# An mLSTM cell and tanh-shrink kernel: gates in three groups, one scaling of v, decay after the sum, transfers and weights in another order

## The chip, the cores and the metric

The kernel runs on one core of one Trainium2 chip. The metric is device time in microseconds (us) of that core, for one execution. A single-core program has no second core to compare with, so a run is called slow only where it lies over 1.5% above the fastest of its kernel. Medians below are of all runs, and a slow one among them is named; ratios, and the verdicts drawn from them, use fast runs alone. The engines are PE (TensorE), PEld (its weight loads), DVE (VectorE), ACT (ScalarE), POOL (GpSimd) and SP (SyncE, which only issues transfers here).

## The reference

An mLSTM cell over 768 tokens, 4 batches and 8 heads of 40, then x @ w_in, g = h - tanh(h), g @ w_out. Cut to what matters:

```python
for t in range(S):
    m_new = max(f_gate[t] + m, i_gate[t])
    f_stab, i_stab = exp(f_gate[t] + m - m_new), exp(i_gate[t] - m_new)
    m = m_new
    C = f_stab * C + i_stab * outer(v[t], k[t])
    n = f_stab * n + i_stab * k[t]
    y[t] = sigmoid(o_gate[t]) * (C @ q[t]) / max(abs(n . q[t]), 1)
# x = y as [3072 tokens, 320 features]
h = x @ w_in                       # 320 x 2048
out = (h - tanh(h)) @ w_out        # 2048 x 320
```

## The kernel before

The sequence is cut into six chunks of 128 tokens. One chunk of one batch is a *unit*: 24 units, n = 4 x chunk + batch. A unit has, on PE, the scores (`ps`, k times q), the products inside the chunk (`ph` from `vs` and `P`), from the second chunk on the product with the carried state (`ph` from `state`), the update of that state (`pc`) and three transposes (`px`) that turn its result into columns of x. Two units make a group of 256 tokens for the large products: up (`ph_up`, x by w_in) and down (`po`, g by w_out). The weights come as 64-bit numbers and are converted to fp32 by DVE and ACT, block by block.

What is emitted for the first twelve units and the first up and down products is decided when the program is built, by a small planner. It holds a list of operations with estimated durations, ranks and dependences, always takes the one that can start first (the lower rank where two can), and emits it. Each engine then runs its instructions in the order emitted. So a wrong estimate costs nothing in correctness, but the engine stands in line behind the instruction that is late.

The planner fills what it believes to be PE idle time with *dummies* (`awake`, a bf16 product of 512 columns that nobody reads), meant to keep the array's clock up:

```python
def idle(t0, t1):
    n = int((t1 - t0) * 0.6 / 0.215)
    if n and not busy:
        awake(n)
```

The gates of chunk 0 are computed at once, those of chunks 1 to 5 together. Their rows lie in the x tiles of later groups:

```python
f_sb, i_sb, m_sb, lf = (... for t in xT[-4:])
load_gates(early)                  # chunk 0, first in the sync queue
...                                # kz, qz, v of two units; then o and k of two units
load_gates(later)                  # chunks 1 to 5
...
first_tokens, _ = gates(0, 1, -2.0, 3.6, in_small)
...
later_tokens, later_states = gates(1, NT, 1.5, 12.0, in_po)
```

v is scaled twice, once for the product inside the chunk and once for the state at its end; the old state is decayed first, and the update added with a mask for the pair of heads that share a product:

```python
scale = ei[:, both, t["c"], t["hs"]]                 # both = two scales
V.tensor_tensor(out=t["vs"][:, both, :, 0:D], in0=v, in1=scale, op=OP.mult)
V.tensor_tensor(out=new, in0=old, in1=eT[:, n, :], op=OP.mult)
...
for i in range(2):
    V.scalar_tensor_tensor(out=new, in0=pc, scalar=own[0:TOP, i:i + 1], in1=new, op0=OP.mult, op1=OP.add)
```

## Time and profile before

| | before |
|---|---|
| median of three runs | 571.06 us (568.33 to 571.93) |
| span of the profiled run | 570.1 us |
| PE busy | 551.2 us, 97% |
| DVE busy | 353.5 us, 62% |
| mean granted PE clock | 0.977 |
| bytes moved | 38.2 MB, 67 GB/s |

PE is the bound, so the number to work with is not its busy share, which counts waiting in the pipeline and half-clock passes as busy. It is the *loss*: the time up to some moment, less the work done by then at undisturbed rates (up product 4.52/24 us each, and so on, as the prediction lists them). Counted so from the trace, the loss before is 24.5 us at 50 us, 33.6 at 70, 33.8 at 100, 36.7 at 190 and 39.6 at the end. The prediction's count of 31.0 at 65.3 us credits PE with 2 us of gates as well, which the curve leaves out, and the last 6.7 us of the curve are the program's tail. Late in the program the curve falls (37.5 at 260 us, 33.0 when PE ends at 563.4), so the prediction's rates are a little too slow there, and losses of the late part are hidden; two kernels' curves can still be compared. The curve of each kernel is used below. Its steps are good to about one us, as an instruction counts when it ends.

### The profile page before, as it was taken

The numbers are of one execution on the slowest core, as the hardware profiler recorded it, in microseconds if no ns is written. First come the engines' busy times: TensorE is split into PE (matmuls) and PEld (weight loads), VectorE is DVE, ScalarE is ACT, GpSimd is POOL, SyncE is SP. The second block draws the span as 40 slices with busy tenths as digits, with TensorE's granted clock in tenths as the row PEclk, the third lists the DMA queues.
The fourth block names the chain that finished last, engine by engine and source line by source line (L and its number), as shares of the span: only waits on it lengthen the run. The fifth ranks groups of instructions, "written<-read, shape, count | busy, mean of one in ns | idle before, by whom it ended". The sixth has DMA issues, their size and how long they took to land.

```text
span 570.1 us, 9133 instructions
## 1 busy us (share of the span) xinstructions
PE 551.2 (97%) x3473; PEld 462.6 (81%) x3476; DVE 353.5 (62%) x769; ACT 179.2 (31%) x436; POOL 34.6 (6%) x69
## 2 busy tenths in 40 slices
PE   8788899999999999999999999999999999999995
PEld 4576687878877777689988988988988989988873
DVE  4789778788875425678656665665664555544421
ACT  2435343364242323313223222322322323232321
POOL 6230202320000000000000000000000000000000
PEclk9789799899999999999999999999999999999999
DMA  7985335453120000212122122111120000000000
GB/s 216 243 244 165 105 104 170 135 175 88 42 87 0 1 0 13 81 37 59 41 65 58 37 69 70 55 62 47 30 65 13 1 23 2 2 24 0 24 0 29
DMA packets 40194, 38.21 MB, mean 67 GB/s; under 512 B 3856, under 2 KB 37712, under 8 KB 40144
## 3 DMA queue, kind: packets, MB, share of 16 engines
q1 hardware_dynamic: 32712, 22.49, 13.7%
q0 software_dynamic: 3296, 10.82, 6.4%
q10 hardware_dynamic: 4136, 4.26, 2.1%
q8 instruction: 29, 0.48, 0.4%
q14 instruction: 21, 0.17, 0.1%
HBM read 33.62 MB, written 3.93 MB: 66 GB/s over the span
## 4 chain that ended last, share of the span: by engine, by line
PE 92%; DMA 3%; ACT 1%; DVE 1%; ACTq 1%; issue 0%; SPq 0%; DVEq 0%
PE ph_up L129 39%; PE pS L129 20%; PE po L129 16%; PE ph L129 9%; PE ps L129 4%; DMA qz<-in_qT 3%; PE pc L129 2%; PE px L133 2%; ACTq L106 1%; ACT q L106 0%; ACT z L106 0%; SPq L288 0%; DVE gt L106 0%; PE gate L129 0%; ACT L106 0%
## 5 line engine op out<-in xcount | busy, mean ns | idle before, releaser
L129 PE MATMUL ph_up<-xT,w_in 128*128 128x256 f32 (+1 forms) x1152 | 248.7, 394 | 2.0 <-ACT xT L106 1.1
L129 PEld LDWEIGHTS ph_up<-xT,w_in 128*128 128x128 f32 (+1 forms) x1152 | 170.4, 190 | 34.9 <-issue 12.2
L106 ACT ACTIVATE z<-ph_up 128x512 f32<-128x512 f32 (+1 forms) x100 | 57.1, 576 | 285.4 <-issue 156.4
L106 DVE SCALAR_TENSOR_TENSOR gt<-ph_up,z 128x512 f32<-128x512 f32 (+1 forms) x100 | 63.5, 663 | 103.0 <-ACT z L106 103.0
L129 PE MATMUL po<-w_out,gt 128*128 128x320 f32 x320 | 99.3, 455 | 2.5 <-DVE gt L106 2.0
L129 PEld LDWEIGHTS po<-w_out,gt 128*128 128x128 f32 x320 | 60.8, 198 | 29.5 <-issue 6.6
L106 DVE TENSOR_TENSOR P<-ps,upto 128x512 f32<-128x512 f32 x48 | 31.5, 684 | 62.3 <-PE ps L129 62.3
L106 ACT ACTIVATE q<-z,tiny 128x512 f32<-128x512 f32 (+1 forms) x100 | 64.9, 701 | 0.9 <-DVE gt L106 0.9
L106 DVE SCALAR_TENSOR_TENSOR gt<-q,gt 128x512 f32<-128x512 f32 (+1 forms) x100 | 63.1, 661 | 0.0
L129 PEld LDWEIGHTS ph<-vs,P 128*128 128x128 f32 x384 | 58.2, 194 | 4.2 <-ACT o L106 0.5
L129 PE MATMUL ph<-vs,P 128*128 128x41 f32 x384 | 57.2, 264 | 0.0
L129 PE MATMUL pS<-wT,s 128*128 128x160 f32 x336 | 52.0, 301 | 0.0
L129 PEld LDWEIGHTS pS<-wT,s 128*128 128x128 f32 x336 | 47.4, 190 | 0.0
L129 PE MATMUL pS<-w_out,gt 128*128 128x160 f32 x224 | 43.7, 315 | 0.0
L129 PEld LDWEIGHTS pS<-w_out,gt 128*128 128x128 f32 x224 | 32.7, 191 | 4.0 <-issue 3.3
L129 PE MATMUL ph<-state,q 80*128 80x82 f32 x160 | 31.4, 278 | 0.0
L129 PEld LDWEIGHTS ps<-qz,kz 40*128 40x128 f32 x384 | 25.4, 187 | 5.8 <-issue 4.0
L129 PE MATMUL ps<-qz,kz 40*128 40x128 f32 x384 | 27.2, 277 | 2.4 <-DMA qz<-in_qT 2.4
L129 PEld LDWEIGHTS ph<-state,q 80*128 80x128 f32 x160 | 26.4, 191 | 2.7 <-issue 0.3
L459 POOL DMA_DIRECT2D w<-in_moe_w_in x40 | 22.8, 576 | 73.5 <-DVE w_e L106 25.2
L106 ACT COPY xT<-px 128x384 f32<-128x384 f32 x24 | 11.4, 476 | 47.6 <-PE px L133 47.6
L129 PEld LDWEIGHTS pc<-vs,k 128*80 128x80 f32 x160 | 19.9, 172 | 3.4 <-issue 0.5
(92 smaller groups left out, 458.5 us busy)
## 6 DMA issues: line engine op xcount, KB each, us to landing
w<-in_moe_w_out POOLq DMA_DIRECT2D x16, 320.0 KB, 4.2
kz<-in_kT SPq DMA_DIRECT2D x48, 80.0 KB
o<-in_o_gate SPq DMA_DIRECT2D x24, 160.0 KB
k<-in_k SPq DMA_DIRECT2D x24, 160.0 KB
out<-ob ACTq DMA_DIRECT2D x24, 160.0 KB
qz<-in_qT SPq DMA_DIRECT2D x44, 80.0 KB
v<-in_v SPq DMA_DIRECT2D x22, 160.0 KB
q<-in_qT SPq DMA_DIRECT2D x40, 80.0 KB
```

Of the source, the lines that this page charges most:

```text
L106: i = method(*args, **kwargs)
L129: return cls.keep(nc.tensor.matmul(*args, **kwargs))
L133: return cls.keep(nc.tensor.transpose(*args, **kwargs))
L459: queue.dma_start(out=to[rows, cols], in_=part)
```

## The change

Its intent: let the first products start earlier, spread the gates, take work off DVE, and let the planner know what dummies and transfers really take. Cut to its core:

```diff
-        LAG = {"T": 0.25, "V": 0.07, "A": 0.12, "S": 1.7, "G": 1.9}
-        RATE = 0.23
+        LAG = {"T": 0.25, "V": 0.07, "A": 0.12, "S": 1.7, "G": 1.9, "N": 1.7}
+        RATE, SHARED = 0.25, 32.4
 ...                                  (each queue has its own transfer time in the plan)
-    f_sb, i_sb, m_sb, lf = (... for t in xT[-4:])
+    f_sb, i_sb, m_sb, lf = (... for t in (w_out[:, 2 * KEPT:], w_in[:, KEPT:]) for i in range(2))
-    load_gates(early)
+    load_gates(0, 2)
-    for name in "ok":
-        for n in range(2):
-            load_unit(n, (name,))
-    load_gates(later)
+    for n in range(2):
+        load_unit(n, ("o",))
 ...
+    CHUNKS = (0, 1, 2, NT)
 ...                                  ("until", "end" and "to end" are gone)
-        V.tensor_tensor(out=t["vs"][:, both, :, 0:D], ...two scales...)
+        V.tensor_tensor(out=to[:, :, 0:D], in0=t["v"], in1=scale..., op=OP.mult)
 ...
-                V.scalar_tensor_tensor(out=new, in0=pc, scalar=own[0:TOP, i:i + 1], in1=new, op0=OP.mult, op1=OP.add)
+            V.tensor_tensor(out=new, in0=pc, in1=old, op=OP.add)
+        V.tensor_tensor(out=new, in0=new if t["c"] else pc, in1=decay, op=OP.mult)
 ...
+    plan_gates(0, -2.0, 3.3, in_small)
+    plan_gates(1, -1.64, 3.3, in_po)
-    later_tokens, later_states = gates(1, NT, 1.5, 12.0, in_po)
+        if n == 2 * B:
+            plan_gates(2, 1.17, 30.0, in_po)
 ...
-            op = plan.add("G", 1.2 if k else 2.8, fetch, (), r, [("w64", held)], at=at, kb=655)
+            op = plan.add("S" if k else "G", 1.5 if k else 2.8, fetch, (), r, [(buffer, held)], at=..., kb=655)
 ...
-        n = int((t1 - t0) * 0.6 / 0.215)
+        n = int((t1 - t0) * 0.9 / 0.43 if t0 < 6.0 else (t1 - t0) * 0.4 / 0.215)
```

Ranks of units and weight blocks change too. The second ring for w_out exists only in the plan: the transfers themselves are still issued by GpSimd.

## The prediction

> **What bounds the kernel now.** I read the page first: busy times, slices and chain.
>
> ```profile
> PE 551.2 (97%) x3473; PEld 462.6 (81%) x3476; DVE 353.5 (62%) x769; ACT 179.2 (31%) x436; POOL 34.6 (6%) x69
> PE   8788899999999999999999999999999999999995
> DVE  4789778788875425678656665665664555544421
> PEclk9789799899999999999999999999999999999999
> PE 92%; DMA 3%; ACT 1%; DVE 1%; ACTq 1%; issue 0%; SPq 0%; DVEq 0%
> ```
>
> PE (TensorE) carries the chain. Two things stand out: VectorE (DVE) is nearly full only in the first slices of 14.25 us each, and PE's granted clock sags there. So I ask how much of PE's time is useful work at the full clock. The chain of waits in order of time gives undisturbed rates (start us, us, what):
>
> ```profile
> 98.51 1.27 PE po L129 x4
> 99.78 1.09 PE ps L129 x16
> ...
> 172.52 4.52 PE ph_up L129 x24
> ...
> 246.81 4.00 PE pS L129 x28
> ...
> 540.94 4.52 PE ph_up L129 x24
> 545.46 4.50 PE po L129 x16
> ```
>
> The counts are from the page's groups: 1152 ph_up x 4.52/24 = 217.0 us; 320 po x 4.50/16 = 90.0; 784 pS (336+224+112+112) x 4.00/28 = 112.0; 384 ps x 1.09/16 = 26.2; ph for 4 units of the first chunk at 1.71 and 20 others at 2.80 = 62.8; 20 updates (pc) at 0.62, the step from 46.14 to 46.76 in the timeline, = 12.4; 24 transposes (px) at 0.42 = 10.1; gates about 2. Sum 532.5 us. The last product ends near 563.4, followed by a tail of 6.7 us (eviction, store, end). So PE loses about 31 us.
>
> Where? At 65.3 us PE has done 48 ph_up (9.0), 24 po (6.8), five score sets (5.5), four first-chunk units (6.8), four updates (2.5), four transposes (1.7) and the gates (2): 34.3 us of work. That is a loss of 31.0 us, all of it. Whatever the change does, it can only gain before about 65 us. Stretches of that opening (columns: stretch, us, then busy us and count for PE, PEld, DVE, ACT, POOL, then clock, DMA share, GB/s):
>
> ```profile
> 12.00:18.00 6.00, 5.78 (x44) 4.68 (x42) 4.25 (x9) 3.74 (x6) 2.29 (x4) 0.72 1.05 290
> 18.00:23.00 5.00, 2.71 (x23) 2.16 (x21) 4.59 (x14) 0.48 (x1) 0.14 (x1) 1.00 0.90 248
> 23.00:28.00 5.00, 4.65 (x31) 3.58 (x33) 1.82 (x5) 2.50 (x5) 2.54 (x5) 0.66 0.86 233
> 28.00:33.00 5.00, 4.29 (x30) 3.08 (x28) 5.00 (x10) 3.14 (x9) 1.10 (x2) 1.00 0.73 192
> 33.00:38.00 5.00, 3.57 (x8) 2.62 (x9) 5.00 (x10) 1.60 (x5) 3.39 (x5) 0.68 0.95 312
> 50.00:55.00 5.00, 4.99 (x28) 3.92 (x29) 5.00 (x9) 3.12 (x5) 0.00 (x0) 1.00 0.37 108
> 55.00:60.00 5.00, 2.16 (x13) 1.29 (x11) 4.93 (x11) 3.98 (x9) 2.42 (x5) 0.87 0.19 52
> 60.00:65.00 5.00, 4.66 (x10) 3.20 (x11) 5.00 (x9) 0.97 (x4) 1.35 (x3) 0.50 0.37 103
> ```
>
> Until 28 us the data is late and engines wait in line; from 28 to 65 us DVE is full except for a stretch at 38 to 43. The timeline shows two knots:
>
> ```profile
> 23.13 1.35 PE L129 MATMUL ps<-qz,kz 40*128 40x128 f32 x16 [2.42 <-DMA qz<-in_qT]
> 26.29 0.68 DVE L106 TENSOR_SCALAR state<-pc,own 80x164 f32<-80x164 f32 x2 [3.18 <-PE pc L129]
> ...
> 49.59 1.53 DVE L106 TENSOR_TENSOR_SCAN xT<-xT,xT,xT 32x640 f32<-32x640 f32 x1
> ...
> 57.92 0.54 PE L129 MATMUL gate<-lfT,upto 128*128 128x160 f32 x2 [1.72 <-DVE lfT L106]
> 59.04 0.90 PE L129 MATMUL gate<-lfT,after 128*128 128x160 f32 x2 [0.58 <-ACT ei L106]
> 60.34 2.50 PE L129 MATMUL po<-w_out,gt 128*128 128x320 f32 x4 [0.39 <-ACT eS L106]
> ```
>
> First, the third unit's queries arrive at 23.1, PE stands, DVE stands behind PE for a state update, and the first weight block, landed at 13.4, is ready only at 27.7. Second, the gates of five chunks at once put 5.7 us of DVE work and two-way waits into PE's order just where DVE is full, and a half-clock window (0.50) follows.
>
> **What the Trainium skill says.** "TensorE: Matmul & The Clock Gate", Part 1: the array runs at half rate until a window of some 3.4 us has been busy, and falls back after an idle one. The trace agrees: 0.50 at 60 to 65 after 2.16 busy us in five. "VectorE: DVE Perf Modes", Mode 1x: two-tensor fp32 operations yield one result a cycle at 0.96 GHz, so 320 elements fewer are 0.33 us; this trace has 0.817 for 640 and 0.481 for 320, a difference of 0.336. "DMA: Bandwidth & Descriptors", Issuing engines are not separate DMA queues: a second issuing queue brings no bandwidth, as all share 16 engines. The share above, 0.9 to 1.05 at 10 to 23 us, fits.
>
> **The change part by part.**
>
> Scaling and state. v is scaled into one copy instead of two: 0.817 to 0.481, minus 0.336 us of DVE for each of 20 units. The state is (k v + old) x decay, two operations of 328 elements at about 0.49 each (row of the old decay, 0.490), in place of 0.490 + 2 x 0.376; minus 0.26. In the first chunk it is one of 0.49 for 0.756; minus 0.27. So 0.6 us a unit, 12 us in all, but only the six preparations (2.0) and four updates (1.1) before 65 us can count: 3.1 us of DVE. Later DVE is at 60% and these gain nothing.
>
> Gates. The "until" sums go: one product, one exponential and one multiply per chunk group. The groups become chunks 0, 1 and 2 to 5. Chunk 1 costs DVE about 2.4 us (scan 0.41, three of 0.36, the rest 0.19 each), early; the last four about 4.6 (scaled between 128 and 640 elements), needed only by the ninth unit. Together 7.0 instead of 5.7: 1.3 more work, but 3.3 less before the knot at 50 us. Between 50.0 and 65.3 PE did 24 ph_up, 8 po and gates, some 8.4 us; 6.9 were lost. I expect 4 of these back. The gate rows also leave the tiles of the later activations.
>
> Transfers. k of the first units and the late gates leave the front of the sync queue (3.04 us of issue for k from 6.25, then gates until 11.3), so the third unit's keys and queries are issued some 5 us earlier than 11.4 and 13.0. The state update and k are put off, so DVE finishes the first block sooner. The first up product starts at 28.59; its x tiles could be there at 21 to 22. I expect it at 23 to 24: 5 us.
>
> Weights. The plan now counts w_out on its own ring with its own buffers, but the diff leaves both fetches issued by the GpSimd queue and the tiles in the same four buffers. So what changes is order, and the plan's belief; the latter may misplace waits. Conversion operations stay 3.41 us of DVE a block. Splitting the ACT step costs nothing.
>
> Dummies. Before, 14 ran from 2.09 to 7.96 and the gate transposes waited for them until 7.89 although their rows were done at 4.5; the new count (0.43 us each) fits the idle time. Perhaps 1 to 2 us on gates and scores, but the first block's landing hides most of it. After 6 us there are fewer, so the clock may sag more.
>
> Sum: 5 (start) + 4 (gate knot, with its half clock) + 2 (of the 3.1 of DVE work, the rest overlapping) - 1.5 (the late gates coming back, waits misplaced, clock) = 9.5 us; from 571 to about 561.
>
> **The rivals.** (a) DVE becomes the opening's bound and lets little through. From 28 to 65 us it is busy 34.6 of 37 (for); but it idles 8.6 between 6 and 28 (against). A bound by sums, an estimate: through the second pair of units DVE needs about 36 us from 10 us on (four units at 3.85, four blocks at 3.41, item work of about 6), while PE has some 33 us of work by then; so a loss of at least 13 us stays however good the order, and likely 17 to 22. Best case thus near 556. (b) The four chunks' gates only move the knot: PE again stands, later. Then only 5 to 6 us are won, 565. (c) The GpSimd queue runs ahead with weights as before (four blocks issued by 15.2 us) and still starves the third unit's queries: the start gains 1 or 2, giving 566. (d) A false wait between gate rows and weights, now in one tile: 570 or more; I see no sign of it, since weight blocks are written and read side by side in this trace.
>
> **Range and chances.** Predicted 561.0 us, 8 in 10 between 554.0 and 567.0. The 2% line is at 559.6 to 559.9, so just below my centre: faster by over 2% 0.41, within 2% 0.56, slower 0.03. Three runs before spread from 568.3 to 571.9, small beside this.
>
> **What would show it.** The first ph_up at 23 to 24 instead of 28.6; scores of the third unit without the 2.4 us wait; no stretch like 55 to 60 with PE at 2.2 of 5; unit scaling rows all of 128x320 at 0.48; PE full from about 50 us on instead of 65; the rest of the program unchanged in length (from PE's steady start to the end within 2 us). I am wrong if the first up product still starts after 27, if a gate wait of several us reappears on PE, or if PE loses time after 80 us, where I expect nothing.

## The result, and the profile after

Ratios here are the mean time of one kernel's fast runs over that of the other's fast runs of the same rounds, so not quite the ratio of the medians that are quoted.

| | before | after |
|---|---|---|
| median | 571.49 us (568.33 to 571.97, 4 runs) | 562.72 us (561.23 to 564.5, 4 runs) |
| ratio | | 0.9858, 95% interval 0.9818 to 0.9899 |
| profiled span | 570.1 us | 559.5 us |
| loss at 50 / 70 / 100 / 190 us / end | 24.5 / 33.6 / 33.8 / 36.7 / 39.6 | 25.9 / 27.0 / 26.6 / 26.2 / 29.1 |

The kernel is 1.4% faster, which is the same at the 2% line, and 1.7 us from the predicted 561.0. The page of the changed kernel, its busy times, the slices of DVE and of the clock, and the shares of the chain:

```profile
PE 546.4 (98%) x3460; PEld 461.2 (82%) x3460; DVE 346.0 (62%) x754; ACT 179.3 (32%) x441; POOL 34.3 (6%) x67
DVE  4699888989854335767656647547556546553421
PEclk9999999999999999999999999999999999999998
PE 95%; DVE 2%; DMA 1%; issue 0%; SPq 0%; ACT 0%
```

Queries no longer appear in the chain (DMA 3% to 1%; what is left are the first unit's keys, for which PE waits 1.22 us at 8.7), and the clock row has lost its dips, though its first 31 us can't be trusted, as is shown next. The same stretches as in the prediction, with the same columns:

```profile
12.00:18.00 6.00, 6.00 (x35) 5.46 (x35) 2.88 (x9) 2.96 (x9) 1.59 (x3) 1.00 1.07 308
18.00:23.00 5.00, 5.00 (x23) 4.51 (x22) 3.03 (x11) 0.36 (x1) 0.00 (x0) 1.00 0.66 218
23.00:28.00 5.00, 5.00 (x25) 2.58 (x22) 4.27 (x8) 3.87 (x8) 1.50 (x3) 1.00 0.54 152
50.00:55.00 5.00, 5.00 (x38) 4.15 (x36) 5.00 (x10) 0.28 (x1) 2.48 (x5) 1.00 0.48 142
55.00:60.00 5.00, 5.00 (x38) 4.17 (x37) 4.93 (x13) 4.80 (x13) 0.19 (x1) 1.00 0.52 168
60.00:65.00 5.00, 5.00 (x53) 4.83 (x52) 3.88 (x12) 0.62 (x3) 0.00 (x0) 1.00 0.25 70
```

From 50 to 65 us the knot is gone: PE ran 13 matmuls in the stretch 55 to 60 before, at 2.16 us busy, and 38 now. But read 12 to 23 with care. PE is full and the clock column says 1.00, yet it did 58 instructions there against 67 before. The timeline of this opening (start, duration, what) shows why:

```profile
14.17 3.63 PE L129 MATMUL ph<-vs,P 128*128 128x41 f32 x16
...
17.84 0.17 DVE L106 SCALAR_TENSOR_TENSOR den<-ph,inv 128x8 f32<-128x8 f32 x1 [1.88 <-PE ph L129]
...
18.45 3.47 PE L129 MATMUL ph<-vs,P 128*128 128x41 f32 x16
...
19.48 0.48 DVE L106 TENSOR_SCALAR w_e<-w 128x640 int32<-128x640 int32 x1
...
24.64 2.08 PE L129 MATMUL ps<-qz,kz 40*128 40x128 f32 x16
...
28.32 3.86 PE L129 MATMUL ph_up<-xT,w_in 128*128 128x256 f32 x12 [0.20 <-DVE w_in L106]
```

The sixteen products of a first unit took 3.63 and 3.47 us. Before, the second of these passes looks like this:

```profile
17.86 1.88 PE L129 MATMUL ph<-vs,P 128*128 128x41 f32 x16
```

So the array ran at half rate until about 31 us. The clock records of this trace begin only with the release at 30.9 us; the column shows 1.00 where there is no record yet. Before, the first release came at 7.5 us.

Where the 10.6 us between the two spans went (loss 39.6 against 29.1), by the two curves: up to 50 us the changed kernel is 1.4 *worse*. From 50 to 70 it gains 8.0 (the old loses 9.1 there, the new 1.1). From 70 to 100 it gains 0.6. From 100 to 190 it gains 3.3, in which the old had two half-clock windows of 3.4 us, at 103.1 and 154.3, and the new none. After 190 nothing differs. But this trace is of the fastest of the changed kernel's four runs, and the only one with a mean clock of 0.997; the other three have 0.989 to 0.991. A second trace (experiment 9) loses 23.6 / 27.9 / 29.1 / 28.4 / 31.4 at the same points: 0.9 better up to 50 us, 4.8 better from 50 to 70.

### The profile page after: what moved, and what is told of

Same layout as the page of the kernel before. It is cut to its first block, busy times and chain, and to the rows that moved or that the text cites. A ratio compares the mean times of both kernels' runs of the same rounds, so it can differ in the third digit from the quotient of the medians.

```text
span 559.5 us, 9108 instructions
## 1 busy us (share of the span) xinstructions
PE 546.4 (98%) x3460; PEld 461.2 (82%) x3460; DVE 346.0 (62%) x754; ACT 179.3 (32%) x441; POOL 34.3 (6%) x67
## 4 chain that ended last, share of the span: by engine, by line
PE 95%; DVE 2%; DMA 1%; issue 0%; SPq 0%; ACT 0%
PE ph_up L129 40%; PE pS L129 20%; PE po L129 15%; PE ph L129 10%; PE ps L129 4%; PE pc L129 2%; PE px L133 2%; DMA kz<-in_kT 1%; DVE gt L106 1%; PE awake L129 0%; DVE P L106 0%; DVE w_e L106 0%; DVE w_in L106 0%; PE gate L129 0%; DVE den L106 0%
## 5 line engine op out<-in xcount | busy, mean ns | idle before, releaser
L129 PE MATMUL po<-w_out,gt 128*128 128x320 f32 x320 | 93.9, 439 | 0.0
L129 PEld LDWEIGHTS po<-w_out,gt 128*128 128x128 f32 x320 | 58.5, 190 | 25.7 <-issue 5.0
L129 PEld LDWEIGHTS ph<-vs,P 128*128 128x128 f32 x384 | 60.5, 202 | 4.7 <-issue 1.2
L129 PE MATMUL ph<-vs,P 128*128 128x41 f32 x384 | 59.7, 272 | 0.0
L129 PE MATMUL ps<-qz,kz 40*128 40x128 f32 x384 | 30.1, 297 | 1.2 <-DMA kz<-in_kT 1.2
L129 PE MATMUL ph<-state,q 80*128 80x82 f32 x160 | 31.2, 276 | 0.0
L129 PEld LDWEIGHTS ps<-qz,kz 40*128 40x128 f32 x384 | 27.4, 205 | 4.1 <-issue 2.7
L106 ACT COPY xT<-px 128x384 f32<-128x384 f32 x24 | 11.4, 476 | 39.6 <-PE px L133 39.6
L129 PEld LDWEIGHTS pc<-vs,k 128*80 128x80 f32 x160 | 17.9, 150 | 4.8 <-DVE state L106 0.7
```

Source lines behind the costliest of these rows:

```text
L106: i = method(*args, **kwargs)
L129: return cls.keep(nc.tensor.matmul(*args, **kwargs))
```

## The experiments

Twelve kernels ran, in four calls of four, four, three and one; each timed beside runs of the kernel before on the same chip. All results were correct. *Undone* means the changed kernel with that part put back; *alone* means the kernel before with that part put in. The theory after the result was that the gates' regrouping gave most of the gain. Its rivals: the dummies' count, the place of the gate rows, the lighter DVE work, or chance in the clock.

### 1. The old dummy count, undone

```diff
-        n = int((t1 - t0) * 0.9 / 0.43 if t0 < 6.0 else (t1 - t0) * 0.4 / 0.215)
+        n = int((t1 - t0) * 0.6 / 0.215)
```

> The changed kernel with the old count of dummy products (0.6/0.215 per us of planned idle time). Theory COLD (formed from the two traces: in the changed kernel the array ran at half clock until 30.9 us, because only 18 dummies run and the small score and intra products do not release the clock): more dummies release the clock at about 7.5 us, the intra sets of units 0 and 1 take 1.9 instead of 3.5 us each, the first up product starts 2 to 5 us before 28.3, and the time falls to 557 to 560. Rival COUNTED (the prediction on record): the old count delays the first gates by some 3 us and costs 1 to 2 us, 563 to 565. Rival NOTHING: the start is bound by transfers and VectorE, 562 to 563.5 with the clock released early all the same.

Measured: 566.53 us median (562.45 to 572.04, 4 runs), ratio to before 0.9869 (0.9761 to 0.9977). One of the four (572.04) is slow. The fast ones average 565.2, some 2 us above the changed kernel's 562.8, with an interval that also holds no difference. Its trace has 33 dummies for 18, but only eight in the opening row of them: the plan's own idle time is shorter there than in the old plan. Its clock was released at 31.3 us, no earlier, and dropped again at 65.5 (6.8 us) and 99.6. The loss at 60 us is 28.5 against 27.3. So the experiment shows that the new count doesn't hurt; it is no test of a warm start.

### 2. The new dummy count, alone

```diff
-        n = int((t1 - t0) * 0.6 / 0.215)
+        n = int((t1 - t0) * 0.9 / 0.43 if t0 < 6.0 else (t1 - t0) * 0.4 / 0.215)
```

> The kernel before with the new count of dummies only. COLD: 14 dummies at the start become fewer, the clock is not released before 20 us or later, and the time rises by 1 to 4 us to 572 to 575. COUNTED: gates run earlier, 569 to 571. NOTHING: 571 to 572 with a late release of the clock.

Measured: 571.34 us (566.66 to 575.5, 20 runs, the one at 575.5 slow), ratio 0.9992 (0.9965 to 1.0019). Nothing, with a narrow interval. In its trace the half clock moved (12.4 to 29.4, 36.3 to 43.1), and the end stayed. The count of dummies by itself is not where the gain lies.

### 3. Two groups of gates, undone

```diff
-    load_gates(0, 2)
+    load_gates(0, 1)
 ...                                   (after the two loads of o)
+    load_gates(1, NT)
-    CHUNKS = (0, 1, 2, NT)
+    CHUNKS = (0, 1, NT)
-    plan_gates(1, -1.64, 3.3, in_po)
     plan_weights(0, 0.08, 3.0)
+    plan_gates(1, 1.5, 12.0, in_po)
-        if n == 2 * B:
-            plan_gates(2, 1.17, 30.0, in_po)
```

> The changed kernel with its gates again in two groups (chunk 0, then chunks 1 to 5 at once, loaded in front and planned as before). Theory KNOT (the loss curves of the two traces differ by 8 us between 50 and 70 us, where the kernel before waited on the gates of five chunks): 4 to 8 us come back, 567 to 571, with a stretch of several us in which PE waits on gates near 45 to 60 us. Rival ORDER (the ranks and loads of the rest did it, the grouping is secondary): 563 to 565. My prediction on record gave this part 4 us.

Measured: 578.95 us (578.26 to 586.99, 4 runs, the one at 586.99 slow), ratio 1.0122 (1.0016 to 1.0229). With all else of the change in place, it is 16 us slower than the changed kernel, and slower than the kernel before. The stretches of its trace:

```profile
50.00:55.00 5.00, 0.93 (x4) 0.53 (x4) 4.14 (x15) 3.37 (x7) 2.02 (x4) 0.85 0.59 177
55.00:60.00 5.00, 5.00 (x32) 4.45 (x33) 3.35 (x8) 2.79 (x7) 0.00 (x0) 0.50 0.39 109
```

and the two instructions of its timeline on either side of the hole:

```profile
49.01 0.50 PE L129 MATMUL gate<-lfT,ones 128*80 128x160 f32 x2
53.50 0.90 PE L133 MATMUL px<-ident,ys 128*128 128x128 f32 x3 [4.00 <-DVE ys L106]
```

PE stands for 4.00 us behind DVE just after the gates of five chunks, and the idle time costs twice: the clock is at half from 53.5 to 70.6 us. Loss from 50 to 70: 11.9 (27.2 to 39.1), where the changed kernel has 1.1. The knot of the kernel before is back, and worse.

### 4. Three groups of gates, alone

In the kernel before: gate rows held in the weight tiles as in the change, chunks 0 and 1 loaded first, the rest loaded by the plan, three calls of `gates`.

```diff
-    f_sb, i_sb, m_sb, lf = (... for t in xT[-4:])
+    f_sb, i_sb, m_sb, lf = (... for t in (w_out[:, 2 * KEPT:], w_in[:, KEPT:]) for i in range(2))
-    load_gates(early)
+    load_gates(0, 2)
-    load_gates(later)
-    first_tokens, _ = gates(0, 1, -2.0, 3.6, in_small)
+    plan_gates(0, -2.0, 3.6, in_small)
+    plan_gates(1, -1.64, 3.6, in_po)
-    later_tokens, later_states = gates(1, NT, 1.5, 12.0, in_po)
+        if n == 2 * B:
+            plan_gates(2, 1.17, 30.0, in_po)
```

> The kernel before with only this of the change: gate rows kept in the weight tiles, chunks 0 and 1 loaded and worked at the start, chunks 2 to 5 as a third group planned from 30 us. KNOT: most of the gain by itself, 563 to 567, and no idle stretch near 55 to 60 us. ORDER: less than a third of it, 568.5 to 571.5. If the early second group crowds the first 15 us, some of it is lost at the start.

Measured: 565.07 us (560.41 to 572.43, 4 runs, the one at 572.43 slow), ratio 0.9865 (0.9742 to 0.9988). By the ratio of the fast runs that is 7.7 us from this part alone, where the whole change has 8.1 (0.9858); with three fast runs the interval reaches from 0.7 to 14.7 us. Experiments 3 and 4 bracket it from both sides.

### 5. DVE as heavy as before, undone

```diff
         V.tensor_tensor(out=to[:, :, 0:D], in0=t["v"], in1=scale.unsqueeze(2)..., op=OP.mult)
+        V.tensor_tensor(out=more, in0=t["v"][:, :, 0:23], in1=..., op=OP.mult)
 ...
-        V.tensor_tensor(out=new, in0=new if t["c"] else pc, in1=decay, op=OP.mult)
+        for i in range(2):
+            half = slice(i, H, 2)
+            V.tensor_tensor(out=new[:, half], in0=..., in1=decay[:, half], op=OP.mult)
```

An extra product of 184 elements stands in for the second scaling, whose full tile did not fit beside the others.

> The changed kernel, same order, with the VectorE time of the old scaling and state given back: a further product of 184 elements (some 0.34 us) behind each scaling of v, and the decay in two halves of 164 elements (0.26 us more). Prediction on record: about 2 us of the gain came from the lighter VectorE; then this run is 2 us slower than the changed kernel, 564 to 566, and PE's loss by 60 us is up by 1.5 to 3 us. Rival: VectorE waits for others often enough that nothing is lost, within 0.7 us of the changed kernel (562 to 563.5).

Measured: 566.08 us (562.46 to 571.39, 16 runs, the one at 571.39 slow), ratio 0.9922 (0.9894 to 0.995). Some 2 to 3 us above the two looks at the changed kernel (562.7, and 564.0 in experiment 9). In its trace the loss at 60 us is 27.6, against 27.3 for the first trace of the changed kernel: almost none of it is direct. The clock dropped at 65.0 us:

```profile
65.00:70.00 5.00, 5.00 (x22) 4.60 (x22) 2.34 (x8) 3.25 (x5) 0.00 (x0) 0.50 0.42 126
```

and that fall and one at 119.7 carry the difference to that trace (loss 29.7 at 70, 31.2 at 190). But the second trace of the changed kernel has two such falls as well (62.0 and 96.1) and is 2.6 us shorter all the same, 2.5 of them by 50 us (its clock was released at 24.5 us, here at 30.9). So the runs show that the added work costs 2 to 3 us, and the traces do not show where.

### 6. Fourteen dummies at the start of the changed kernel

```diff
-    busy = []
+    busy, first = [], [14]
 ...
+        if first:
+            n = first.pop()
```

> The changed kernel with 14 dummies in a row at the very start (some 5.9 us) in place of 5, everything else the same. Theory COLD: the clock is released at 6 to 8 us instead of 30.9[...], intra sets of units 0 and 1 take 1.9 instead of 3.5 us, loss by 30 us falls by 2 to 4 us, time 558 to 561. Rival GATES: the first gates wait behind the dummies until 8 us, and that eats it: 562 to 564. Rival FALLS BACK: the clock is released but drops again in the windows filled by scores and intra products alone, as in the kernel before (14.4, 24.6, 34.8 us), gain under 1.5 us.

Measured: 563.7 us (561.39 to 565.12, 6 runs), ratio 0.9856 (0.9803 to 0.9908). The first release now came at 7.2 us, but the clock dropped again from 14.0 to 24.2, and the first up product started at 26.5 instead of 28.3. The loss at 50 us is 23.0 for 25.9; then a window at half from 61.8 to 68.6 took 3.3 back. It ends where the changed kernel ends.

### 7. The second ring made real

```diff
-                        [(...moe_w_out...) for i in range(2)], nc.gpsimd))
+                        [(...moe_w_out...) for i in range(2)], nc.sync))
```

> The changed kernel with the second ring made real: w_out fetched by the sync queue, as the plan assumes, instead of the GpSimd queue. If the plan's mistake costs something (misplaced waits, my prediction's minor item): 1 to 3 us faster, 559 to 562. If the ring is no bottleneck: within 1 us. Rival: the sync queue, which waits in order for buffers of the units, delays the weights or is delayed by them, 565 to 572.

Measured: 562.93 us (560.35 to 566.87, 6 runs), ratio 0.9837 (0.9779 to 0.9896). No difference. That agrees with the Trainium skill, "DMA: Bandwidth & Descriptors", Issuing engines are not separate DMA queues, which has the engines that issue share the same transfer engines. So the plan's mistake about the ring costs nothing that can be measured. It is no test of the rival that the GpSimd queue's weights starve the units' transfers, as w_in still runs ahead on that queue; that rival is answered by the changed kernel's trace, where PE waits for no transfer after 8.7 us.

### 8. The place of the gate rows, alone

```diff
 (as experiment 4, but)
-    CHUNKS = (0, 1, 2, NT)
+    CHUNKS = (0, 1, NT)
-    load_gates(0, 2)
+    load_gates(0, 1)
 ...                                   (after the loads of o and k)
+    load_gates(1, NT)
+    plan_gates(1, 1.5, 12.0, in_po)
```

> The kernel before with only the place of the gate rows changed (into the weight tiles, so the later activation tiles are free early), but still two groups of chunks. Theory GROUPING: the place alone gives nothing, 569.5 to 573, and the gates of five chunks still hold PE near 55 to 60 us. Rival PLACE: the freed tiles are what helps, 564 to 568 as with three groups.

Measured: 571.47 us (566.95 to 575.38, 14 runs), ratio 0.9993 (0.9958 to 1.0028). Nothing. The stretch 55 to 60 of this kernel, and below it that of experiment 4:

```profile
55.00:60.00 5.00, 2.20 (x10) 1.45 (x11) 4.93 (x12) 3.88 (x8) 2.67 (x5) 0.83 0.30 91
```

```profile
55.00:60.00 5.00, 3.53 (x22) 2.72 (x19) 4.93 (x12) 4.38 (x12) 2.67 (x5) 1.00 0.44 138
```

With two groups PE has 2.20 busy us in the stretch, as before the change (2.16); with three it has 3.53, and the clock never drops after 19.9 us in that trace. So it is the grouping, and neither the tile in which the rows lie nor a false wait between rows and weights.

### 9. The changed kernel again

No edit, a second look.

> The changed kernel itself, unchanged, for the spread of its time and a second trace. Theory PHASE (formed from the traces so far: a granted window of 3.4 us that falls wholly on scores and intra products drops the clock to half for one or two windows, and where the windows fall differs from run to run): its own trace and times vary, median 562 to 565, and this trace may show a half-clock stretch near 60 to 70 us that the first one did not have. Rival FIXED: the clock pattern belongs to the program, the second trace repeats the first with no drop after 30.9 us.

Measured: 563.96 us (561.81 to 570.9, 6 runs of which the one at 570.9 is slow), ratio 0.9857 (0.9803 to 0.9911). The time repeats; the trace doesn't quite. Here the clock was released at 24.5 us, two windows sooner, the first up product started at 27.0 and the loss at 50 us is 23.6, not 25.9. But the clock fell to half from 62.0 to 68.8, and at 96.1. The stretches around the first fall:

```profile
58.60:62.00 3.40, 3.40 (x38) 3.23 (x38) 2.28 (x8) 0.00 (x0) 0.00 (x0) 1.00 0.17 47
62.00:65.40 3.40, 3.40 (x19) 3.40 (x18) 1.14 (x3) 2.05 (x4) 0.00 (x0) 0.50 0.55 161
```

In the 3.4 us before the fall PE was busy for 3.40 and did 38 matmuls; nothing idled. What it did, from the timeline:

```profile
59.00 0.43 PE L129 MATMUL ph<-state,q 80*128 80x82 f32 x2
59.27 0.58 PE L129 MATMUL ph<-vs,P 128*128 128x41 f32 x4
59.77 1.16 PE L129 MATMUL ps<-qz,kz 40*128 40x128 f32 x16
```

Only scores and a unit's small products, of 41 to 128 columns, and no up or down product. The window before the fall at 96.1 is of the same kind, and so are those before the falls at 103.1 and 154.3 in the kernel before (99.7 to 103.1 has 1.1 us of scores and 2.3 of small products). That kernel's falls at 24.6, 34.8 and 58.7 are of another kind: PE was busy for 1.47, 1.36 and 1.03 us of the 3.4 before them. The first trace of the changed kernel had such a mix too, at 61.6 to 65.0 us, but with 0.19 us of transposes in it, and kept its clock; and the kernel before kept it after 133.8 to 137.2 with nothing but small products. So the line is thin, and whether a window falls on a stretch of small products depends on how the grid of 3.4 us happens to lie (in the kernel before the clock changes at 7.5, 14.4, 17.8, 24.6, 28.0, 34.8 and 38.3 us, each 3.4 or 6.8 after the last). Nor is it told apart whether the kind of product counts or idle time inside small ones that the profile does not show: one of 41 columns takes 0.118 us (1.88/16), one of 256 columns 0.188 (4.52/24). That gave a new theory, which experiment 10 tests: the remaining falls come from long stretches of small products, and a plan that breaks them up loses none.

### 10. Large products between the small ones

In the planner, once 1.6 us of small PE work has gone out in a row, the next large product that can start at the same time goes first (operations of rank 100 and more are up and down products):

```diff
-                t, _, _, op = min(((t, op["rank"], op["serial"], op) for op ...
+                t, _, _, op = min(((t, -9.0 if op["engine"] == "T" and op["rank"] >= 100.0 and self.small > 1.6 else op["rank"], op["serial"], op) for op ...
                 if op["engine"] == "T":
+                    self.small = 0.0 if op["rank"] >= 100.0 else self.small + op["us"]
```

> The changed kernel with one more rule in its planner: after 1.6 us of scores, intra products and updates on TensorE, an up or down product that is ready goes first. Nothing else changes. Theory PHASE: no half-clock stretch between 40 and 200 us, so median 1 to 3 us below the changed kernel of the same rounds, 560 to 562, with less spread. Rival FIXED or ORDER: within 1 us, or slower by 1 to 3 us because units are finished later.

Measured: 559.72 us (558.28 to 561.45, 6 runs), ratio 0.9784 (0.9738 to 0.9831). Faster than before by 2.2%, though the interval from 1.7 to 2.6% leaves open whether by over 2%; with experiment 11 the best of all kernels here. The stretches and one line of the timeline show the rule at work:

```profile
60.00:65.00 5.00, 5.00 (x42) 4.68 (x42) 3.88 (x12) 0.42 (x2) 0.00 (x0) 1.00 0.22 65
65.00:70.00 5.00, 5.00 (x47) 4.32 (x46) 3.80 (x11) 3.63 (x6) 0.00 (x0) 1.00 0.41 121
```

```profile
62.42 1.32 PE L129 MATMUL po<-w_out,gt 128*128 128x320 f32 x4
```

A down product stands at 62.4 us amid the small ones, and the trace has no half-clock window between 30.7 us and the tail. Its loss at 190 us is 26.5, that of the changed kernel in the same call 28.4. All six of its runs lie below the fastest of that kernel's in the same call (561.45 against 561.81), though the two intervals overlap. That the mechanism is the clock is seen not only in one trace. The mean clock of all six runs is 0.997, which is what the fall in the tail leaves by itself (half of 3.4 us in 559.7); of the nine fast runs of the changed kernel in both looks only two have 0.997 (561.23 and 561.81 us, the fastest of each look), and the others 0.989 to 0.993. In the call of experiments 9 and 10 the mean clock of the fast runs is 0.9918 against 0.997, which is worth about 2.9 us of 562 (an estimate), of the 3.8 us between their mean times.

### 11. Both: large products between, and fourteen dummies

Edits 6 and 10 together.

> The same with the 14 dummies at the start as well. If the gain of 3.2 us by 60 us that the run with 14 dummies showed was real and only lost again to a half-clock stretch at 61.8 to 68.6 us, it is kept here: 557 to 560, over 2% below the kernel before. Rival: VectorE takes its place as the bound after the start, 560 to 562.

Measured: 559.74 us (558.21 to 560.49, 6 runs), ratio 0.9783 (0.9738 to 0.9829). The loss of its trace is 1.7 us lower at the end (27.6 against 29.3), and its median the same to 0.02 us. The dummies released the clock at 5.1 us, and it was back at half from 12.0 to 29.0 all the same. So they buy nothing that lasts.

### 12. k of the first two units in front again

On top of 10:

```diff
-    for n in range(2):
-        load_unit(n, ("o",))
+    for name in "ok":
+        for n in range(2):
+            load_unit(n, (name,))
```

> The interleaved version (559.7 us) with k of the first two units loaded in front of the third unit's keys and queries, as in the kernel before; the planner lays out the rest around that. My prediction on record gave the moved transfers 5 us at the start. If that holds, this run is 3 to 6 us slower, 563 to 566, with the third unit's scores and the first up product later. Rival, from the loss curves (the changed kernel loses no less than the one before by 50 us): within 1.5 us of 559.7.

Measured: 566.32 us (564.49 to 567.77, 22 runs), ratio 0.9934 (0.9915 to 0.9953), with 6.6 us lost against experiment 10 (by medians of different calls). But not at the start, where the prediction put the worth of this part: the third unit's scores start at 24.45 and the first up product at 28.1, where experiment 10 has 28.8 and the changed kernel 28.3. It is lost between 50 and 70 us (loss 26.3 to 33.0), where the late gates wait and the clock falls:

```profile
56.31 0.45 PE L129 MATMUL gate<-lfT,ones 128*80 128x128 f32 x2 [1.18 <-ACT ei L106]
```

The edit changes the plan's whole order, not the transfer alone, so it shows how sensitive the plan is. What k's transfer costs by itself is left open.

## Why the prediction was right, and where it wasn't

**The total and the range** held: 561.0 predicted, 562.7 and 564.0 measured in two looks, and the 2% line was rightly seen as near. The sum inside was wrong in three of its terms, and that these cancelled is luck: in the first pair of traces the start gave -1.4 us for the 5 forecast, the gate knot 8.0 for 4, and the stretch from 100 to 190 us 3.3 for nothing.

**"Start: 5 us"** failed. The step that failed is "the state update and k are put off, so DVE finishes the first block sooner ... I expect it at 23 to 24". The queries' wait of 2.42 us went, as said. But the third unit's scores start at 24.64, later than 23.13, and the first up product at 28.32, later by the prediction's own test than 27. The block had landed by 12.8 us; its conversion began at 19.48, because DVE's order put the first unit's gating ahead of it, and that gating waited 1.88 us on PE passes at half clock; the second unit's gating, in the midst of the conversion, waited another 1.59. Behind this lies a reading of the clock. The prediction had it fall after an idle window, found that the trace agrees, and gave its sagging a share of 1.5 us. But of the six falls in that trace before the tail, three (14.4, 103.1 and 154.3) follow 3.4 us in which PE was busy throughout, and its own line for 12 to 18 us has PE busy for 5.78 of 6 at a clock of 0.72. That a full PE would run at half until 24 to 31 us it did not foresee. Between two traces of the same kernel this alone moves the loss at 50 us by 2.3 (23.6 and 25.9), so the cost of a cold start against the old start isn't sharper than that.

**"Gate knot: 4 us"** was right in mechanism, its half-clock window included, and too small. The term "6.9 lost, 4 back" measured 8.0 in the first pair of traces, and 4.8 in the second look, where the clock fell at 62.0. Regrouping alone gives 7.7 with a wide interval (experiment 4), and without it the rest of the change is worth less than nothing: 579 us (experiment 3). The prediction let 2.9 of the 6.9 stay lost; in the first trace after, the late gates cost PE no idle time and the whole stretch from 50 to 70 us loses 1.1.

**"2 of the 3.1 us of DVE work"**: the scaling rows are all 128x320 at 0.48 us as foreseen, the state's two operations about 0.49 each:

```profile
L106 DVE TENSOR_TENSOR vs<-v,ei x24: 470/484/488, 12.5 to 473.7; 128x320 f32<-128x320 f32 x24
```

(The prediction's 0.33 us for 320 elements is an estimate from the rate that it cites; its trace had 0.336.) DVE work put back cost 2 to 3 us (experiment 5), so the size is near. But only 0.3 us of it is seen directly by 60 us, and how the rest came about stays open.

**"From PE's steady start to the end within 2 us"** was off. Loss after 100 us was 5.8 before and 2.5 after; the difference of 3.3 lies between 100 and 190, where before had two falls of the clock and the first trace after none. The claim that the change can only gain before 65 us ("a loss of 31.0 us, all of it") failed for the same reason. It came of the balance: the curve of the kernel before still climbs from 33.3 at 65.3 us to 37.5 at 260, and as the rates are too slow for the late part, it is back at 33.0 when PE ends, so the two sums agreed and the later loss was not seen. It is not a sure gain: the second trace after had a fall at 96.1.

**"The late gates coming back"** did not happen: they run from 53.4 to 55.7 us in the changed kernel, without idle time on PE. So rival (b), a knot that only moves, falls. Rival (c), the GpSimd queue that starves the queries, falls by the trace after, where the third unit's scores wait for no transfer, and rival (d), a false wait, by experiment 8. Rival (a), a floor near 556, was not reached by any kernel: the best trace still loses 27.6 us, tail included, and spans 558.0; the fastest run of all took 558.21.

**Open:** why fourteen dummies warm the clock and don't shorten the median; what exact mix in a window makes the clock fall; what k's transfer is worth; where the 2 to 3 us of the lighter DVE work arise; and what the ranks, the plan's transfer times and the dropped "until" sums are worth by themselves, as no run put back one of these alone.

## What to carry to other kernels

Split a preparation by when its results are needed, and put it where no full engine stands in line for it; here computing four late chunks' gates apart from the second's was worth most of the gain, and its absence turned the other parts into a loss. Where PE is the bound, count useful work at full rate against time, since a busy PE at half clock looks the same in the busy row, and look at what fills the windows ahead of each fall of the clock. In an order planned at build time, mix large products among the small ones: that step, three lines, took the kernel from 1.4% to 2.2% below the time before.

## What the Trainium skill lacked or had wrong

- "TensorE: Matmul & The Clock Gate", Part 1: it has the clock fall after an idle window, and tells of another kernel where short idles between groups of products made it swing. Here it also fell to 0.50 after a window in which the profile counts PE busy for 3.40 of 3.40 us, with scores and unit products only (58.6 to 62.0 us in the second look), and a rule that puts a large product in between left no fall between 30.7 us and the tail in its trace. The page doesn't say which products count as busy.
- The same part has the clock released after about 3.4 us of sustained work. Here PE was busy for all of 12 to 27.5 us, with such small products, transposes and a few dummies, and was released only at 30.9 us (24.5 in the second look), with passes of 3.63 and 3.47 us that take 1.88 at the full clock.
- No page has it that this profile's clock row reads 1.00 before the first clock record. In the changed kernel it does until 30.9 us, so its mean of 0.997 is too high, and the length of a known pass is the better sign.
